# Loading w_down's 64 partitions with six DMAs of 4, 4, 4, 2, 2 and 48 rows in place of eight DMAs of 8 rows

## The chip, the cores and the metric

The kernel runs on one core of a Trainium2 chip. The time is the device time of one execution in microseconds, and the figure to compare is the median of several executions. Before the change it is 2533.44 us (three runs, 2533.29 to 2534.53). A profiled execution also gives a span, from the first to the last instruction, which is a little shorter than the device time.

## The reference

One token is sent through two blocks, and the results are mixed by a gate. Block A is attention over a cache of 65,536 positions with 32 heads of 128; block B is a SwiGLU feed-forward with F = 1792:

```python
q = (x @ wq).reshape(B, Sq, H, Dh).transpose(0, 2, 1, 3)          # 32 heads of 128, one query
p = softmax(einsum("bhqd,bhkd->bhqk", q, k_cache) * Dh ** -0.5)
a = einsum("bhqk,bhkd->bhqd", p, v_cache)  ->  (1, 1, 4096) @ wo   # wo 4096 x 512
b = (silu(x @ w_gate) * (x @ w_up)) @ w_down                       # w_down 1792 x 512
g = sigmoid((x * gate_w).sum(-1, keepdims=True))
out = g * a + (1 - g) * b
```

Everything is bf16. The two caches are 32 x 65536 x 128 values each, 537 MB each, so more than 98% of the bytes that the kernel reads are K and V. w_down is 1.8 MB.

## The kernel before, in words

**Tiles.** A head's 65,536 positions are cut into G = 4 chunks of 16,384, so there are N = 128 chunks. A chunk of K or V is one tile of 128 partitions with 128 positions of 128 values in each: 32 KB per partition, 4 MB in all, loaded by one DMA (`load`, line 108). All large tiles come from one ring of five buffers (`ring`, `SLOTS = 5`), and the same ring holds, at the start, `wq_t`, the two matrices of the feed-forward's input (`gu_t`), and w_down (`wd_t`); at the end it holds the second half of wo.

**The steps.** The loop at line 355 goes through `steps`, one K chunk n and, four or more steps later, one V chunk v. For a K chunk VectorE multiplies K by the query (line 240) and halves the products three times by adding (line 244), until 16 partial sums per position are left; TensorE adds these up with an identity matrix (`scores`, line 254). When a head's four chunks are there, the maximum, the exponentials and the row sum follow (lines 266 to 288). For a V chunk TensorE multiplies the probabilities by V (`values`, line 302).

**The feed-forward.** It is done in the first steps: `feed_forward_in` after step 1 (`gu_ps`, line 176), `feed_forward_mid` in step 2, `feed_forward_out` in step 3. In `feed_forward_mid` TensorE rearranges the hidden vector from 128 partitions of 14 to 64 partitions of 28 (line 202) and then multiplies it by w_down in 28 matmuls (`b_ps`, line 209). w_down stands on 64 partitions for that, each with 28 rows of 512: 28 KB in one run, both in memory and in the tile. These 28 matmuls need all of w_down.

**The order of the DMAs.** All loads but x's are issued by SyncE, in the order of the program, on one hardware queue whose packets are carried by 16 DMA engines. A load of a ring buffer waits until the buffer's last reader is done. Besides, the DMAs take turns on eight completion semaphores, so that each DMA is issued only when the eighth one before it has landed. The order at the start is: wq, K chunk 0 in two halves, K chunk 1, w_gate, w_up, gate_w, two DMAs of w_down (`load_wd(0, 1)`), K chunk 2, six DMAs of w_down (`load_wd(2, ..., 7)`, line 359), K chunk 3, a piece of wo, K chunk 4, V chunk 0, and so on. The buffer of w_down is taken next by K chunk 5.

**w_down's DMAs before.** `load_wd` (line 142) takes rows `lo, lo + 4, ..., lo + 28` for each of eight values of `lo`, so each DMA moves 8 partitions that lie 4 apart, 28 KB each.

Of the kernel before, what the change touches and what calls it, by code (L numbers as in the profile page):

```python
# [25 lines left out]
def kernel(  # L26
# [75 lines left out]
    def load(dst, cache, n, name, cuts=(0, NB)):  # L102
        h, g = divmod(n, G)
        t = big(name)
        view = t.rearrange("p (j d) -> p j d", d=Dh)
        src = cache[0, h, g * NB * P : (g + 1) * NB * P, :].rearrange("(p j) d -> p j d", j=NB)
        for a, b in zip(cuts[:-1], cuts[1:]):
            nc.sync.dma_start(out=view[:, a:b, :], in_=src[:, a:b, :])
        dst[n] = view
# [31 lines left out]

    def load_wd(*which):
        for i in which:
            lo = (0, 1, 2, 3, 32, 33, 34, 35)[i]
            part = slice(lo, lo + 29, 4)
            nc.sync.dma_start(out=wd_sb[part], in_=wd_rows[part])

    with nc.allow_non_contiguous_dma(reason="small"):
# [8 lines left out]
    def load_wo_end(cuts):  # L157
        t = big("wo_t")[:, : (H - WH) * D].rearrange("p (h n) -> p h n", n=D)
        rows = A_wo[WH * P :, :].rearrange("(h p) n -> p h n", p=P)
        for a, b in zip(cuts[:-1], cuts[1:]):  # L160
            nc.sync.dma_start(out=t[:, a:b, :], in_=rows[:, a:b, :])
        wo_end.append(t)

    def load_wo(g):
        wo_tiles[g] = wo_pool.tile([P, WG, D], bf16, name="wo_sb")
        rows = A_wo[g * WG * P : (g + 1) * WG * P, :]
        nc.sync.dma_start(out=wo_tiles[g], in_=rows.rearrange("(h p) n -> p h n", p=P))

    def feed_forward_in():

        gu_ps = psum_m.tile([P, 2 * FT], f32, name="gu_ps", tag="misc")
        for w in range(2):
            cols = wgu_sb[:, w].rearrange("p t (m c) -> p t c m", c=FT)
            for ft in range(FT):
                for t in range(KT):
                    nc.tensor.matmul(
                        gu_ps[:, w * FT + ft : w * FT + ft + 1],
                        lhsT=cols[:, t, ft, :],
                        rhs=xT[:, t : t + 1],
                        start=(t == 0),  # L180
                        stop=(t == KT - 1),
                    )
        gu_sb = consts.tile([P, 2 * FT], f32, name="gu_sb")
        nc.scalar.activation(out=gu_sb, in_=gu_ps, func=ACT.Copy)
        eg = consts.tile([P, FT], f32, name="eg")
        nc.scalar.activation(out=eg, in_=gu_sb[:, :FT], func=ACT.Exp, scale=-1.0)
        return gu_sb, eg

    def feed_forward_mid(gu_sb, eg):
        nc.vector.tensor_scalar_add(eg, eg, 1.0)  # L190
        nc.vector.reciprocal(eg, eg)
        hprod = consts.tile([P, FT], f32, name="hprod")
        nc.vector.tensor_tensor(out=hprod, in0=gu_sb[:, :FT], in1=eg, op=ALU.mult)
        hT = consts.tile([P, FT], bf16, name="hT")
        nc.vector.tensor_tensor(out=hT, in0=hprod, in1=gu_sb[:, FT:], op=ALU.mult)
        xg = consts.tile([P, KT], f32, name="xg")
        nc.vector.tensor_tensor(out=xg, in0=xT, in1=gwT, op=ALU.mult)
        xs = consts.tile([P, 1], f32, name="xs")
        nc.vector.tensor_reduce(out=xs, in_=xg, axis=AXIS.X, op=ALU.add)
        h_ps = psum_m.tile([HP, GT], f32, name="h_ps", tag="misc")  # L200
        for r in range(2):
            nc.tensor.matmul(
                h_ps[:, r * FT : (r + 1) * FT], lhsT=ident_b[:, r::2], rhs=hT, start=True, stop=True
            )
        h2 = consts.tile([HP, GT], bf16, name="h2")
        nc.scalar.activation(out=h2, in_=h_ps, func=ACT.Copy)
        b_ps = psum_m.tile([1, D], f32, name="b_ps", tag="misc")
        for t in range(GT):
            nc.tensor.matmul(  # L209
                b_ps, lhsT=h2[:, t : t + 1], rhs=wd_sb[:, t, :], start=(t == 0), stop=(t == GT - 1)  # L210
            )
        g_ps = psum_m.tile([P, 1], f32, name="g_ps", tag="misc")
        nc.tensor.matmul(g_ps, lhsT=ones_f, rhs=xs, start=True, stop=True)
        eg2 = consts.tile([P, 1], f32, name="eg2")
        nc.scalar.activation(out=eg2, in_=g_ps, func=ACT.Exp, scale=-1.0)
        return b_ps, eg2
# [13 lines left out]
    def products(n, a=0, b=NB):  # L230

        h = n // G
        K = K_tiles[n][:, a:b, :]
        qb = q_bc[:, h * Dh : (h + 1) * Dh]
        q_rep = bass.AP(
            tensor=qb.tensor,
            offset=qb.offset,
            ap=[list(qb.ap[0]), [0, b - a], [1, Dh]],
        )
        yield nc.vector.tensor_tensor(out=K, in0=K, in1=q_rep, op=ALU.mult)  # L240
        half = Dh
        while half > WIDTH:
            half //= 2
            yield nc.vector.tensor_tensor(  # L244
                out=K[:, :, 0:half], in0=K[:, :, 0:half], in1=K[:, :, half : 2 * half],
                op=ALU.add,
            )
# [15 lines left out]
    def row_max(h):  # L263

        m = small.tile([P, 1], f32, name="m")
        nc.vector.tensor_reduce(out=m, in_=S_tiles[h], axis=AXIS.X, op=ALU.max)  # L266
        diag = small.tile([P, P], f32, name="diag")
        nc.scalar.activation(out=diag, in_=ident_f, func=ACT.Copy, scale=m)  # L268
        mT_ps = psum_m.tile([P, P], f32, name="mT_ps", tag="misc")
        nc.tensor.matmul(mT_ps, lhsT=ones_f, rhs=diag, start=True, stop=True)  # L270
        return mT_ps

    def exponentials(h, mT_ps):
        top = small.tile([P, 1], f32, name="top")
        nc.vector.tensor_reduce(out=top, in_=mT_ps, axis=AXIS.X, op=ALU.max)  # L275
        bias = small.tile([P, 1], f32, name="bias")
        nc.scalar.activation(out=bias, in_=top, func=ACT.Copy, scale=-scale)
        P_tiles[h] = ppool.tile([P, NBH], bf16, name="P_sb")
        nc.scalar.activation(  # L279
            out=P_tiles[h], in_=S_tiles[h], func=ACT.Exp, bias=bias, scale=scale,  # L280
            accum_out=rowsum[:, h : h + 1],
        )
        del S_tiles[h]
# [71 lines left out]
    for n, v in steps:  # L355
        if n is not None and n > 1:
            load(K_tiles, A_k_cache, n, "K_t")
        if n == 2:
            load_wd(2, 3, 4, 5, 6, 7)
        if n == 3:  # L360
            load_wo(0)
        if v is not None:
            if v % (WG * G) == 2 * G and v // (WG * G) + 1 < WH // WG:
                load_wo(v // (WG * G) + 1)
            load(V_tiles, A_v_cache, v, "V_t", (0, NB) if v < N - 2 else (0, 64, NB) if v < N - 1 else (0, 32, 64, 96, 112, NB))
            if v == N - 1:
                load_wo_end((0, 4, 8, 12, 14, 16))
        if n == 2:
            ff = feed_forward_mid(*ff)
        halves = (0, NB // 2)  # L370
        vector = iter(()) if n is None else products(n)
        if n == 0:
            vector = (i for a in halves for i in products(n, a, a + NB // 2))
        top_of = None
        if n is None:
            top_of = H - 1 if S_tiles else None
        elif n % G == 0 and n > 0:
            top_of = n // G - 1
            vector = (i for a in halves for i in products(n, a, a + NB // 2))
        if top_of is not None:  # L380
            next(vector, None)
            mT_ps = row_max(top_of)
            next(vector, None)
            exponentials(top_of, mT_ps)
        for _ in vector:
            pass
        if n == 1:
            ff = feed_forward_in()
        if n == 3:
            feed_forward_out(*ff)  # L390
        if tot_ps is not None:
            weight(*tot_ps)
            tot_ps = None
        if done is not None:
            head_column(done, head_copy(done))
        if v is not None:
            values(v)
        if top_of is not None:
            tot_ps = top_of, total(top_of)
        if n is not None:  # L400
            scores(n)
        if done is not None and done < WH:
            project(done)
        done = v // G if v is not None and v % G == G - 1 else None
# [40 lines left out]
```

## Time and profile before

| | |
|---|---|
| median of three runs | 2533.44 us |
| the profiled execution | 2534.51 us, span 2532.6 us |
| VectorE busy | 2175.5 us (86%) |
| TensorE busy | 1742.4 us (69%) |
| read from memory | 1087.64 MB, 429 GB/s over the span |
| V loads of 4096 KB, issue to landing (median) | 29.1 us |
| K loads of 4096 KB, issue to landing (median) | 35.3 us |
| 28 matmuls with w_down | 12.1 us, from 60.35 us on |

In the views of the profile, "L302" is line 302 of the kernel, "DVE" is VectorE, "PE" TensorE, "ACT" ScalarE and "SPq" the queue of SyncE, which issues the DMAs. "V_t<-in_A_v_cache_dram" reads: tile V_t from the input A_v_cache. A DMA's "landing" is the moment at which its last engine has reported completion. Each engine that takes part in a DMA reports it with a small packet of four bytes of its own, and these marks, with their times, are in the trace's records beside the packets of data. In the view by windows, the columns after each engine's busy time give the granted clock of TensorE, the mean busy share of the 16 DMA engines, and GB/s.

### The profile page before, as it was taken

The numbers are of one execution on the slowest core, as the hardware profiler recorded it, in microseconds if no ns is written. First come the engines' busy times: TensorE is split into PE (matmuls) and PEld (weight loads), VectorE is DVE, ScalarE is ACT, GpSimd is POOL, SyncE is SP. The second block draws the span as 40 slices with busy tenths as digits, with TensorE's granted clock in tenths as the row PEclk, the third lists the DMA queues.
The fourth block names the chain that finished last, engine by engine and source line by source line (L and its number), as shares of the span: only waits on it lengthen the run. The fifth ranks groups of instructions, "written<-read, shape, count | busy, mean of one in ns | idle before, by whom it ended". The sixth has DMA issues, their size and how long they took to land.

```text
span 2532.6 us, 15260 instructions
## 1 busy us (share of the span) xinstructions
PE 1742.4 (69%) x6738; PEld 712.1 (28%) x6738; DVE 2175.5 (86%) x784; ACT 75.9 (3%) x207; POOL 0.7 (0%) x6
## 2 busy tenths in 40 slices
PE   4677666776677666676776677667666776677679
PEld 2222222222222222222222223222222232222223
DVE  7998888888888999998888888888888888888860
ACT  1000000000000000000000000000000000000000
POOL 0000000000000000000000000000000000000000
PEclk7677777777777676677777777777777777777779
DMA  9999999999999999999999999999999999999998
GB/s 415 433 433 430 433 433 433 432 430 435 432 432 434 431 433 432 432 433 433 432 434 433 432 434 433 432 432 434 432 431 434 433 430 434 434 431 433 434 432 339
DMA packets 42884, 1088.63 MB, mean 430 GB/s; under 512 B 4737, under 2 KB 8834, under 8 KB 9090
## 3 DMA queue, kind: packets, MB, share of 16 engines
q1 hardware_dynamic: 42674, 1087.66, 99.7%
q8 instruction: 53, 0.87, 0.1%
q14 instruction: 13, 0.11, 0.0%
q10 hardware_dynamic: 144, 0.00, 0.0%
HBM read 1087.64 MB, written 0.00 MB: 429 GB/s over the span
## 4 chain that ended last, share of the span: by engine, by line
DMA 68%; PE 22%; DVE 10%; issue 1%; ACT 0%; DVEq 0%; SPq 0%
DMA V_t<-in_A_v_cache_dram 61%; PE O_ps L302 20%; DMA K_t<-in_A_k_cache_dram 5%; DVE K_t L240 5%; DVE K_t L244 5%; PE S_ps L254 1%; DMA wo_t<-in_A_wo_dram 1%; DMA wq_t<-in_A_wq_dram 0%; PE qg_ps L117 0%; DVE m L266 0%; PE oh_ps L323 0%; PE a_ps L335 0%; PE a_ps L227 0%; ACT P_sb L279 0%; DVE top L275 0%
## 5 line engine op out<-in xcount | busy, mean ns | idle before, releaser
L302 PE MATMUL O_ps<-V_t,P_sb 128*4 128x512 bf16 x4096 | 1157.3, 453 | 496.8 <-DMA V_t<-in_A_v_cache_dram 494.3
L240 DVE TENSOR_TENSOR K_t<-K_t,q_bc 128x16384 bf16<-128x16384 bf16 (+1 forms) x160 | 1117.2, 6983 | 254.4 <-DMA K_t<-in_A_k_cache_dram 232.9
L244 DVE TENSOR_TENSOR K_t<-K_t 128x4096 bf16<-128x4096 bf16 (+3 forms) x480 | 1030.9, 2148 | 14.3
L302 PEld LDWEIGHTS <-P_sb 128*4 128x4 bf16 x4096 | 393.9, 97 | 1241.0 <-issue 897.5
L254 PE MATMUL S_ps<-K_t,ident_b 128*128 128x128 bf16 x2048 | 466.0, 394 | 107.0 <-DVE K_t L244 106.9
L254 PEld LDWEIGHTS <-ident_b 128*128 128x128 bf16 x2048 | 227.6, 115 | 330.0 <-issue 140.2
L323 PE MATMUL oh_ps<-ident_f,O_sb 4*128 4x1 f32 x256 | 57.9, 343 | 74.1 <-ACT O_sb L315 74.1
L323 PEld LDWEIGHTS oh_ps<-ident_f,O_sb 4*128 4x128 f32 x256 | 55.2, 314 | 83.7 <-ACT O_sb L315 78.9
L270 PE MATMUL mT_ps<-diag,ones_f 128*128 128x128 f32 x64 | 23.6, 468 | 79.8 <-ACT diag L268 79.8
L268 ACT ACTIVATE diag<-ident_f,m 128x128 f32<-128x128 f32 x32 | 12.8, 401 | 2099.3 <-DVE m L266 2099.3
L317 DVE COPY O_sb<-O_ps 4x256 f32<-4x256 f32 x1 | 0.4, 414 | 52.1 <-ACT O_sb L315 52.1
L270 PEld LDWEIGHTS mT_ps<-diag,ones_f 128*128 128x128 f32 x64 | 14.7, 285 | 95.6 <-ACT diag L268 95.6
L266 DVE TENSOR_REDUCE m<-S_ps 128x1 f32<-128x512 f32 x32 | 21.9, 683 | 7.4 <-PE S_ps L254 7.4
L315 ACT ACTIVATE O_sb<-O_ps 4x512 f32<-4x512 f32 (+1 forms) x32 | 18.1, 566 | 131.0 <-PE O_ps L302 131.0
L279 ACT ACTIVATE P_sb<-S_ps,bias 128x512 bf16<-128x512 f32 x32 | 22.0, 687 | 1.0
L117 PE MATMUL qg_ps<-wq_t,X_bc 128*128 128x512 bf16 x32 | 8.6, 436 | 13.2 <-DMA wq_t<-in_A_wq_dram 13.2
L293 DVE RECIPROCAL recip<-tot_ps 128x1 f32<-128x1 f32 x32 | 5.1, 160 | 12.2 <-PE tot_ps L288 12.2
L209 PE MATMUL b_ps<-wd_t,h 64*1 64x512 bf16 x28 | 12.1, 629 | 4.3 <-DMA K_t<-in_A_k_cache_dram 4.3
L288 PEld LDWEIGHTS tot_ps<-rowsum,ones_f 128*128 128x128 f32 x64 | 9.5, 188 | 14.0 <-issue 14.0
L288 PE MATMUL tot_ps<-rowsum,ones_f 128*128 128x1 f32 x64 | 12.2, 260 | 0.0
L330 ACT ACTIVATE oT<-oh_ps,rg 128x1 bf16<-128x1 f32 x32 | 8.4, 263 | 76.6 <-PE oh_ps L323 76.6
L227 PE MATMUL a_ps<-b_sb,ones_f 1*1 1x512 f32 x2 | 1.9, 1032 | 12.1 <-ACT b_sb L226 12.1
(42 smaller groups left out, 73.8 us busy)
## 6 DMA issues: line engine op xcount, KB each, us to landing
K_t<-in_A_k_cache_dram SPq DMA_DIRECT2D x127, 4096.0 KB, 35.3
V_t<-in_A_v_cache_dram SPq DMA_DIRECT2D x126, 4096.0 KB, 29.1
wq_t<-in_A_wq_dram SPq DMA_DIRECT2D x1, 4096.0 KB
K_t<-in_A_k_cache_dram SPq DMA_DIRECT2D x2, 2048.0 KB, 16.8
V_t<-in_A_v_cache_dram SPq DMA_DIRECT2D x2, 2048.0 KB
V_t<-in_A_v_cache_dram SPq DMA_DIRECT2D x3, 1024.0 KB, 29.4
wo_sb<-in_A_wo_dram SPq DMA_DIRECT2D x4, 512.0 KB, 17.3
gu_t<-in_B_w_gate_dram SPq DMA_DIRECT2D x1, 1792.0 KB
```

Of the source, the lines that this page charges most:

```text
L209: nc.tensor.matmul(b_ps, lhsT=h2[:, t : t + 1], rhs=wd_sb[:, t, :], start=(t == 0), stop=(t == GT - 1))
L240: yield nc.vector.tensor_tensor(out=K, in0=K, in1=q_rep, op=ALU.mult)
L244: yield nc.vector.tensor_tensor(out=K[:, :, 0:half], in0=K[:, :, 0:half], in1=K[:, :, half : 2 * half], op=ALU.add,)
L254: nc.tensor.matmul(S_tiles[h][:, g * NB : (g + 1) * NB], lhsT=ident_b, rhs=K_tiles[n][:, :, c], start=(c == 0), stop=(c == WIDTH - 1),)
L266: nc.vector.tensor_reduce(out=m, in_=S_tiles[h], axis=AXIS.X, op=ALU.max)
L268: nc.scalar.activation(out=diag, in_=ident_f, func=ACT.Copy, scale=m)
L270: nc.tensor.matmul(mT_ps, lhsT=ones_f, rhs=diag, start=True, stop=True)
L279: nc.scalar.activation(out=P_tiles[h], in_=S_tiles[h], func=ACT.Exp, bias=bias, scale=scale, accum_out=rowsum[:, h : h + 1],)
L288: nc.tensor.matmul(tot_ps, lhsT=ones_f, rhs=rowsum[:, h : h + 1], start=True, stop=True)
L302: nc.tensor.matmul(O_tiles[h], lhsT=P_tiles[h][:, g * NB + j : g * NB + j + 4], rhs=V_tiles[n][:, j : j + 4, :], start=(g == 0 and j == 0) ...
L315: nc.scalar.activation(out=O_sb[:, :cut], in_=O_ps[:, :cut], func=ACT.Copy)
L323: nc.tensor.matmul(oh_ps, lhsT=O_sb[:, c * Dh : (c + 1) * Dh], rhs=ident_f[0:4, c : c + 1], start=(c == 0), stop=(c == 3),)
```

## The change

w_down's 64 rows are cut in another way: rows 48 to 51, 52 to 55 and 56 to 59 by a DMA of four rows each, rows 60 and 61, and 62 and 63, by a DMA of two rows each, and rows 0 to 47 by one DMA of 48. The first two (48 to 51 and 52 to 55) stand where the first two stood, ahead of K chunk 2, and the other four stand behind it. The same bytes go to the same places in the tile, and nothing else in the kernel differs; each of the engines has the same instructions in the same order, apart from SyncE's two issues fewer.

```diff
     def load_wd(*which):
         for i in which:
-            lo = (0, 1, 2, 3, 32, 33, 34, 35)[i]
-            part = slice(lo, lo + 29, 4)
+            part = slice(*((48, 52), (52, 56), (56, 60), (60, 62), (62, 64), (0, 48))[i])
             nc.sync.dma_start(out=wd_sb[part], in_=wd_rows[part])
...
         if n == 2:
-            load_wd(2, 3, 4, 5, 6, 7)
+            load_wd(2, 3, 4, 5)
```

## The prediction

> **What bounds the kernel now.** I read the head of the page, its forty slices and its chain first, then the table of DMA queues and issues, then the stretch from 0 to 100 us in order of time, then the last 30 us in narrow windows, and last the trace's own packet and semaphore records, which the page does not print and whose numbers I give in words.
>
> ```profile
> span 2532.6 us, 15260 instructions
> PE 1742.4 (69%) x6738; PEld 712.1 (28%) x6738; DVE 2175.5 (86%) x784; ACT 75.9 (3%) x207; POOL 0.7 (0%) x6
> DMA  9999999999999999999999999999999999999998
> DMA packets 42884, 1088.63 MB, mean 430 GB/s; under 512 B 4737, under 2 KB 8834, under 8 KB 9090
> q1 hardware_dynamic: 42674, 1087.66, 99.7%
> q8 instruction: 53, 0.87, 0.1%
> DMA 68%; PE 22%; DVE 10%; issue 1%; ACT 0%; DVEq 0%; SPq 0%
> ...
> V_t<-in_A_v_cache_dram SPq DMA_DIRECT2D x126, 4096.0 KB, 29.1
> wd_t<-in_B_w_down_dram SPq DMA_DIRECT2D x8, 224.0 KB
> ```
>
> No compute engine is full (VectorE 86%), while queue q1 fills 99.7% of 16 DMA engines for the whole span: the time is bytes over the rate of the DMA engines, and an average of 430 GB/s hides which engine is last. A 32 KB packet takes 1213 ns in nearly every record, one of w_down's 28 KB packets 1062 ns in all 64: 27.0 GB/s per engine, 16 times 27 = 432. So a row of w_down costs the engine that carries it 1.06 us, and the question is which engine ends last.
>
> How many engines a DMA uses can be counted: q1 has 4465 four-byte packets, the completion marks. 275 loads of 128 rows at 16 each, eight of 8 rows at 8 each and the one-row output make 4400 + 64 + 1 = 4465. So eight rows go to eight engines, one row each. It is the same eight every time: the K load before w_down's two first pieces lands on all sixteen within 0.73 us, the K load issued at 43.20 us lands on eight engines at 60.1 to 60.5 us and on the other eight at 68.4 to 70.0 us. The 8.3 us between are 8 rows x 1.06 = 8.5 us.
>
> That lead stays to the end. The last V piece (issued 2494.42) lands at 2507.0 (2 engines), 2513.8 to 2514.9 (6), 2515.4 to 2515.6 (4), 2516.2, 2519.8, 2522.6 and 2523.7. Followed back, the first eight are those without w_down. The rest of the spread is q8: each of its 53 instruction fetches of 16 KB stretches a 32 KB packet from 1213 to about 1700 ns, and the lengths repeat with a period of eight, so eight engines take them in turn, 6 or 7 each, and lose some 7 us: six of the eight without w_down and two with it, which are the last two. The windows of the tail show that few engines set the end (share times 16 is the number still moving data):
>
> ```profile
> core 0: us, PE busy (x) PEld busy (x) DVE busy (x) ACT busy (x) POOL busy (x), PEclk, DMA share, GB/s
> 2507.00:2513.00 6.00, 6.00 (x30) 2.34 (x29) 0.00 (x0) 0.00 (x0) 0.00 (x0) 1.00 0.90 379
> 2519.00:2522.00 3.00, 3.00 (x15) 1.19 (x14) 0.00 (x0) 0.00 (x0) 0.00 (x0) 1.00 0.23 88
> 2525.70:2527.90 2.20, 2.20 (x15) 1.34 (x14) 0.23 (x1) 0.26 (x1) 0.00 (x0) 1.00 0.16 53
> ```
>
> From 2519 to 2522 us 0.23 x 16, three to four engines, are left; from 2525.7 two; the last mark is at 2529.1, and the output follows.
>
> **The change, part by part.** Times are against the profiled execution, 2534.51 us (span 2532.6 and 1.9 around it); it lies 1.1 us above the median of 2533.44, and I add the difference to the median.
>
> Issue. Two of eight DMA issues on SyncE go, 2 x 0.62 us (the issues from 22.98 to 42.46 us). Cost nothing: SyncE waits there anyway, each of these issues for the DMA eight earlier on its semaphore. The K load behind them goes out at about 42 instead of 43.20 us, while 10 us of the K load before it is still to come.
>
> ```profile
> 21.86 0.34 SPq L108 DMA_DIRECT2D K_t<-in_A_k_cache_dram  x1
> 22.98 20.11 SPq L146 DMA_DIRECT2D wd_t<-in_B_w_down_dram  x6
> 43.20 0.37 SPq L108 DMA_DIRECT2D K_t<-in_A_k_cache_dram  x1
> ...
> 54.01 8.69 DVE L240 TENSOR_TENSOR K_t<-K_t,q_bc 128x16384 bf16<-128x16384 bf16 x1 [0.80 <-DMA K_t<-in_A_k_cache_dram]
> 60.35 12.10 PE L209 MATMUL b_ps<-wd_t,h 64*1 64x512 bf16 x28 [4.28 <-DMA K_t<-in_A_k_cache_dram]
> ```
>
> Rows per engine. By the counts above (128 rows on 16 engines, 8 on 8, 1 on 1) I take 4 rows on four engines, 2 on two, 48 on sixteen with three each. With the first engines always the same: engines 0 and 1 carry 3 + 2 + 3 = 8 rows, as now; 2 and 3 carry 6; 4 to 7 carry 3; 8 to 15 carry 3 instead of none. By rows alone that is 0, -2.1, -5.3 and +3.2 us. [...]
>
> Where the rows land. Now the eight rows of a piece lie four partitions apart (0, 4, ... 28), and in the large loads each engine writes eight rows of its own, so no record shows two engines writing neighbouring rows. After the change four engines write four neighbouring rows (48 to 51) at once, while the K stream goes on. Bound below: they do not disturb each other, 1.06 us per piece. [...] The nearest row for two streams on one path is the fetch beside a 32 KB packet: 1213 becomes 1700, the two add up and do not overlap. As every packet size runs at the same 27 GB/s, I hold that for a path's limit and take turns. For engines 0 and 1 that is 3 x 5.3 + 2 x 3.2 (two engines and a third) + at most 8.5 (eight rows of the 48 go to each low group) = 30.8 us; I take 28.5, since strangers' rows arrive partly while these engines are held elsewhere. With no K rows in the way it is 3 x 4.25 + 2 x 2.1 + 3.2 = 20.2 us. Today it is 8.5. So +20.0 us for engines 0 and 1 (11.7 to 22.3), some 16 to 18 for 2 and 3, 3 to 7 for the others.
>
> [...]
>
> What waits for that. The K load of step 2 lands at 65 to 69 instead of 53.9 us and that of step 3 at about 90 instead of 70, so VectorE, which starts on them at 54.01 and 70.67, stands still for about 19 us; it idles 233 us for K loads in all, and catches up. w_down is whole at about 80 instead of 60.3 us; the 12.1 us of b_ps on TensorE end at about 92, and behind them the scores of step 2 and the K load that takes w_down's buffer (issued at 72.48 now). Cover: engines 0 and 1 then still hold that K load's two predecessors and end them at about 110, so 18 us are to spare; beyond that every microsecond would be one of the end. The engines that are ahead run dry, at no cost: the last one sets the landing.
>
> Sum. An engine with w_down and without fetches is 8.2 us ahead of the last one (2515.5 against 2523.7). If engines 0 and 1 are such, the end moves by 20.0 - 8.2 = +11.8 us (bounds 3.5 and 14.1): 2533.4 + 11.8 = 2545.2 us.
>
> **The rivals.**
> 1. Turns as above, but one of engines 0 and 1 takes the fetches: +20.0, 2553.4 us (bounds 2545.1 and 2555.7). For it: two of eight are so. Against it: the records carry no engine numbers. With the engine at 2519.8 among them it is +16.
> 2. Faster: no turns, and the two last engines are among 4 to 7. They shed five rows: 5.3 us, the end 2528.1. The eight without w_down go from at most 2514.9 to 2518.1, under 2523.7 - 5.3 = 2518.4, so this gain is whole. It decides if a four-row piece takes less than about 1.5 us. For it: engine load is what bounds the kernel. Against it: the sharing row above.
> 3. No change: no turns, and the last engine is 0 or 1, which carries eight rows before and after: 2533.4; among 2 and 3, 2531.3. The change then does what it says, on engines that do not set the end.
> 4. Turns that are worse than equal, holding up other packets too: above 2556.
>
> **How the numbers follow.** Forecast 0.42; rival 1 0.33; rival 2 0.10; rival 3 0.10; rival 4 0.05. The time is that of the forecast, 2545 us. From 2533 (rival 3) to 2556 (end of rival 1) the range leaves out rivals 2 and 4 and a part of 3, under 0.2. The forecast alone: 2537 to 2548. A measurement of this kernel can tell about 0.2%, 5.1 us. Faster 0.10 (rival 2), same 0.12 (rival 3 and the low edge of the forecast), slower 0.78.
>
> **What the profile after would show.** Right: packets of w_down of 3 to 5 us instead of 1062 ns; the marks of the K load of step 3 spread over some 25 us; b_ps starting near 80 us; VectorE idle ahead of the products of steps 2 and 3; at the end only two to four engines moving data for more than 10 us. Wrong: 1062 ns in all 64 packets (turns fall; rivals 2 or 3, told apart by whether the last marks come 5 us sooner); a spread at step 3 that closes later, if the engines held up find slack I don't see.

## The result and the profile after

The changed kernel takes 2547.43 us (median of four runs, 2546.80 to 2548.38) against 2533.36 us before (four runs): a ratio of 1.0050, 95% interval 1.0039 to 1.0062, or 14.1 us more. The forecast was 2545 us, 2533 to 2556.

The head of the page of the changed kernel, and its rate in forty slices of 63.7 us:

```profile
span 2546.6 us, 15257 instructions
PE 1734.5 (68%) x6738; PEld 710.7 (28%) x6738; DVE 2175.8 (85%) x784; ACT 75.9 (3%) x207; POOL 0.7 (0%) x6
...
DMA  9999999999999999999999999999999999999998
GB/s 339 381 434 429 435 431 434 431 434 430 435 431 433 433 431 435 431 434 432 434 433 432 434 430 434 433 432 433 432 434 431 434 432 432 436 430 433 433 433 372
```

The 16 DMA engines are as busy as before, and the loss is all in the first two slices: 339 and 381 GB/s, then 430 and more to the end. (339 and 381 against 432 over 63.7 us each are 13.7 + 7.5 = 21 us; the start of the program costs 2.8 us of it in both kernels.) So an engine that is busy there moves less: its packets take longer.

Narrower windows of that stretch, first the kernel before, then the changed one (the last two columns are the busy share of the DMA engines and GB/s):

```profile
40.00:50.00 10.00, 5.88 (x99) 5.82 (x98) 9.93 (x3) 0.41 (x2) 0.00 (x0) 0.50 1.04 441
50.00:55.00 5.00, 2.77 (x13) 1.60 (x13) 4.03 (x9) 0.00 (x0) 0.00 (x0) 0.50 0.99 427
55.00:75.00 20.00, 15.72 (x47) 5.47 (x46) 19.90 (x5) 0.36 (x2) 0.00 (x0) 0.50 1.02 435
75.00:80.00 5.00, 1.47 (x7) 0.61 (x5) 4.96 (x2) 0.00 (x0) 0.00 (x0) 0.50 0.98 419
```

```profile
40.00:50.00 10.00, 5.74 (x96) 5.68 (x96) 9.93 (x3) 0.41 (x2) 0.00 (x0) 0.50 1.07 153
50.00:55.00 5.00, 2.91 (x14) 1.69 (x14) 2.91 (x8) 0.00 (x0) 0.00 (x0) 0.50 0.99 423
55.00:75.00 20.00, 0.94 (x6) 0.33 (x4) 7.69 (x1) 0.19 (x1) 0.00 (x0) 0.50 1.00 179
75.00:80.00 5.00, 1.02 (x3) 0.36 (x4) 4.97 (x2) 0.00 (x0) 0.00 (x0) 0.50 0.97 396
```

From 40 to 50 us run the first two pieces of four rows, from 50 to 55 only K chunk 2, and from 55 us on the other four pieces, whose last mark comes at 78.8 us. With the pieces the sixteen engines together move 153 and 179 GB/s; between them, 423. I use one figure for this below, the *loss per engine*: from 40 to 84 us, the bytes short of 432 GB/s, divided by 432, with each packet counted by the part of it that lies in that time (the table counts a packet whole in the window where it begins). It is 0.2 us before and 19.1 us after (in this table, (432 - 153) x 10 / 432 = 6.5 and (432 - 179) x 20 / 432 = 11.7).

In order of time, the changed kernel's waits for that:

```profile
42.62 0.35 SPq L108 DMA_DIRECT2D K_t<-in_A_k_cache_dram  x1
67.31 8.69 DVE L239 TENSOR_TENSOR K_t<-K_t,q_bc 128x16384 bf16<-128x16384 bf16 x1 [14.23 <-DMA K_t<-in_A_k_cache_dram]
78.98 12.10 PE L208 MATMUL b_ps<-wd_t,h 64*1 64x512 bf16 x28 [23.04 <-DMA wd_t<-in_B_w_down_dram]
88.60 8.69 DVE L239 TENSOR_TENSOR K_t<-K_t,q_bc 128x16384 bf16<-128x16384 bf16 x1 [4.55 <-DMA K_t<-in_A_k_cache_dram]
91.11 0.33 SPq L108 DMA_DIRECT2D K_t<-in_A_k_cache_dram  x1
```

VectorE stands still for 14.23 + 4.55 = 18.8 us ahead of chunks 2 and 3, b_ps starts at 78.98 instead of 60.35 us, and the load that takes w_down's buffer goes out at 91.11 instead of 72.48 us. From 80 us on the rate is whole again, so that load was not late.

**Who was held.** The packets of w_down take 3.5 us in the median (1.06 to 4.68), against 1.06 before. But the engines that have nothing to do with a piece are held too: beside the first piece's four packets, begun at 40.3 to 40.5 us, stand twelve 32 KB packets begun at 40.3 to 40.7, and these take 3.6 to 4.9 us instead of 1213 ns; the longest K packet of this stretch takes 5.4 us. The marks carry no engine number; which engine is which is read from the rows it carries and from its lag, which can be followed from load to load. K chunk 2, which has only the first two pieces (engines 0 to 3) ahead of it, landed before the change at 50.4 to 50.9 us on the eight engines without w_down; now eleven engines land it between 57.4 and 58.9 us. K chunk 3 lands at 82.0 to 88.5 us; before at 60.1 to 60.5 on eight engines and 68.4 to 70.0 on eight. So every engine lost 14 to 22 us, and the spread between them fell from 9.9 to 6.5 us. Most of the difference is rows. Taking the marks in order (the twelve first as the engines that now have three rows, then two with six, then two with eight), and counting 1.06 us for each row gained or shed, what is left on the mean is 19.0 us for engines 8 to 15, 19.0 for 4 to 7, 19.1 for 2 and 3, and 19.5 for 0 and 1: all sixteen were held alike.

**The end.** The last V piece landed at 2507.0 to 2523.7 us, on the mean of the sixteen engines at 2515.2; it now lands at 2527.5 to 2537.6, 2533.9 on the mean. The mean is 18.7 us later, the last engine only 13.9: it was 8.5 us behind the mean and is 3.7 us behind it now. The change does even out the engines, by 4.8 us, and pays 18.7 us for it. The windows of the tail of the changed kernel show it:

```profile
2533.00:2536.00 3.00, 3.00 (x16) 1.17 (x15) 0.00 (x0) 0.00 (x0) 0.00 (x0) 1.00 0.77 288
2541.00:2542.50 1.50, 1.50 (x8) 0.57 (x8) 0.00 (x0) 0.26 (x1) 0.00 (x0) 1.00 0.40 130
```

Shortly before the last mark (2543.0 us) 0.40 x 16, about six engines, still move data; at that distance from the end one or two did before.

### The profile page after: what moved, and what is told of

Its sections match the earlier page's. It is cut to its first block, busy times and chain, and to the rows that moved or that the text cites. A ratio compares the mean times of both kernels' runs of the same rounds, so it can differ in the third digit from the quotient of the medians.

```text
span 2546.6 us, 15257 instructions
## 1 busy us (share of the span) xinstructions
PE 1734.5 (68%) x6738; PEld 710.7 (28%) x6738; DVE 2175.8 (85%) x784; ACT 75.9 (3%) x207; POOL 0.7 (0%) x6
## 4 chain that ended last, share of the span: by engine, by line
DMA 69%; PE 21%; DVE 9%; issue 1%; ACT 0%; SPq 0%; DVEq 0%
DMA V_t<-in_A_v_cache_dram 61%; PE O_ps L301 20%; DMA K_t<-in_A_k_cache_dram 6%; DVE K_t L239 4%; DVE K_t L243 4%; DMA gwT<-in_gate_w_dram 2%; PE S_ps L253 1%; DMA wo_t<-in_A_wo_dram 1%; DVE m L265 0%; PE oh_ps L322 0%; PE a_ps L334 0%; ACT P_sb L278 0%; PE a_ps L226 0%; SPq L108 0%; DVE top L274 0%
```

## The experiments

Theory 1, formed from the trace after: engines that write neighbouring partitions at the same time crowd there, and the crowd slows all sixteen engines. Its rivals: that few engines per DMA, neighbouring rows in memory, or the 48-row piece alone cost the time, and that only the writers are held, in turns, as the prediction had it. The edits that take out a line with `lo`, and the last one, are against the kernel before, the others against the changed kernel (the one with `pad` in place of `h2` adds to the run ahead of it); where the number of pieces changes, the calls of `load_wd` change with it and are not shown. Where an expectation says to which partitions an engine's K rows go, that is my assumption: the records name neither engines nor rows. Each ratio below is against runs of the kernel before on the same chip (medians 2534.4 to 2534.6 us).

### Small pieces with their rows four apart

```diff
-            part = slice(*((48, 52), (52, 56), (56, 60), (60, 62), (62, 64), (0, 48))[i])
+            part = slice(*((48, 64, 4), (49, 64, 4), (50, 64, 4), (51, 64, 4), (0, 48))[i])
```

> w_down as four 4-row pieces whose rows lie four apart (48, 52, 56, 60 and so on) and the same 48-row piece. In the changed kernel the total rate falls to 131-175 GB/s from 40 to 50 us, while the first two 4-row pieces run (6.7 us lost), and to 118-262 from 55 to 75 us (11.8 us lost). Theory 1, crowding: engines that write neighbouring partitions together slow all sixteen engines. Then 40 to 50 us is back at about 430 GB/s, only the 48-row piece still loses some 5 us, and the time is 2533 to 2539 us. Rival A, few engines: a DMA on four engines is itself the cost, wherever its rows land. Then 40 to 50 us stays under 200 GB/s, four pieces lose 13 us, and the time is 2545 us or more. Rival B, turns as predicted: only the engines that write into a foreign group are held, 7 to 15 us on engines 0 to 3, and the total rate never falls under 300 GB/s: 2533 to 2548 us.

Measured: 2542.2 us, ratio to before 1.0032 (1.0019 to 1.0045), 7.8 us more. Its windows:

```profile
40.00:50.00 10.00, 5.83 (x98) 5.77 (x97) 9.93 (x3) 0.41 (x2) 0.00 (x0) 0.50 1.03 317
50.00:55.00 5.00, 2.82 (x14) 1.60 (x14) 2.99 (x8) 0.00 (x0) 0.00 (x0) 0.50 1.15 306
55.00:75.00 20.00, 3.27 (x12) 1.15 (x11) 12.55 (x2) 0.19 (x1) 0.00 (x0) 0.50 0.98 245
```

No theory had it whole. The same number of engines with the same bytes loses 3.0 us from 40 to 52 us where neighbouring rows lost 7.1 in that time, so few engines are not the whole cause. But 317 is not 430, where theory 1 had no loss. The small number of engines alone doesn't make the 3.0 us: the run of `Which engines end last` below, whose pieces are four rows four apart on four engines as well, but at rows 0 to 15 and 32 to 47 of the tile, loses 0.3 us in all. Nor do rows 48 to 63 alone: the kernel before writes them four apart too, in pieces on eight engines, and loses 0.2 us. It is the two together, and why isn't shown. The loss per engine is 13.4 us.

### Large piece with its rows four apart

```diff
-            part = slice(*((48, 52), (52, 56), (56, 60), (60, 62), (62, 64), (0, 48))[i])
+            part = slice(*((48, 52), (52, 56), (0, 48, 4), (56, 60), (60, 62), (62, 64), (1, 48, 4), (2, 48, 4), (3, 48, 4))[i])
```

> The three 4-row and two 2-row pieces as in the change, rows 0 to 47 in four pieces of 12 rows that lie four apart. Theory 1: the small pieces keep their loss (6.7 us from 40 to 50 us, some 6 more behind K chunk 2), the large ones lose nearly nothing: 2541 to 2546 us. Rival C, the 48-row piece is what costs: the small pieces show no loss and the time is 2533 us or less.

The first of the four large pieces stands ahead of K chunk 2 here.

Measured: 2544.4 us, ratio 1.0042 (1.0027 to 1.0057), 10.0 us more; 151 GB/s from 40 to 50 us, 274 from 55 to 75; loss 14.2 us per engine. The small pieces keep their loss; the 48-row piece is not the only cause. Rows four apart are cheaper here too, since the loss is 4.9 us less than the change's.

### The 48-row piece alone

```diff
-    load_wd(0, 1)
...
-            load_wd(2, 3, 4, 5)
+            load_wd(0)          # part = slice(0, 48)
```

> The 48-row piece of the change alone, behind K chunk 2; rows 48 to 63 aren't loaded and the products use rows 0 to 31. It tells the small pieces' share of the 19.1 us that the changed kernel lost per engine (16 engines, against 432 GB/s) from the large one's. By the difference of the runs so far (13.4 us lost with four spaced small pieces, 3.0 of it from 40 to 52 us for two of them) the 48 rows alone lose about 7 us, the small ones 12. Every engine then spends 3.2 + 7 us, against 8.5 of engines 0 to 7 before: the last ones end 2 us later, 2535 to 2537 us. If the loss is from small pieces that hold up the large one: under 3 us lost, and 2531 us or less.

Measured: 2537.92 us, ratio 1.0013 (1.0004 to 1.0022); the loss is 8.3 us per engine, where 7 was expected, and it begins with the piece (40 to 50 us at 428 GB/s, 50 to 55 at 167). So of the change's 19.1 us the large piece makes some 8 by itself and the five small ones, by difference, some 11, though these carry a quarter of the bytes.

### Neighbouring partitions, rows far apart in memory

```diff
             part = slice(*((48, 52), (52, 56), (56, 60), (60, 62), (62, 64), (0, 48))[i])
+            rows = slice(*((0, 64, 16), (1, 64, 16), (2, 64, 16), (4, 64, 32), (5, 64, 32), (0, 48))[i])
-            nc.sync.dma_start(out=wd_sb[part], in_=wd_rows[part])
+            nc.sync.dma_start(out=wd_sb[part], in_=wd_rows[rows])
```

> The changed kernel, but the five small pieces take rows of w_down that lie far apart in memory (0, 16, 32, 48; 1, 17, 33, 49; 2, 18, 34, 50; 4, 36; 5, 37) and still write the neighbouring partitions 48 to 63; so b is computed with wrong rows. If the crowd is at the partitions written: 108-154 GB/s again from 40 to 48 us and about 14 us over the kernel before. If it is neighbouring rows in memory: 40 to 48 us near 430 GB/s, and 6 to 10 us less than the changed kernel.

Measured: 2548.15 us, ratio 1.0057 (1.0043 to 1.0071), 13.6 us more; 142 GB/s from 40 to 44 us and 104 from 44 to 48; loss 21.8 us. Nothing is won by taking the rows apart in memory: what matters is where they are written. Why the loss is 2.7 us larger than the change's isn't shown.

### Eight engines on neighbouring rows

```diff
-            lo = (0, 1, 2, 3, 32, 33, 34, 35)[i]
-            part = slice(lo, lo + 29, 4)
+            part = slice(8 * i, 8 * i + 8)
```

> Eight DMAs of 8 neighbouring rows (0 to 7, 8 to 15, ...): the same eight engines and the same bytes as before the change, but two groups with four writers each, and the K rows of that group's engine as a fifth. Theory 2, pace of the slowest: while a piece runs, all sixteen engines move at a quarter to a fifth of their rate; 8 x 3.2 to 4.2 us = 25 to 34 us lost by every engine, those without w_down too: 108 GB/s and less in each piece, K chunk 3 lands 25 us later on all, 2559 to 2567 us. Rival B, turns: only engines 0 to 7 lose 25 us, the other eight land K chunk 3 at 60 us as before, and 16 engines together stay above 230 GB/s; the time is the same, about 2559 us, so the records decide.

Measured: 2553.53 us, ratio 1.0075 (1.0061 to 1.0088), 19.0 us more; loss 17.3 us. Its windows:

```profile
40.00:50.00 10.00, 5.85 (x98) 5.79 (x98) 9.93 (x3) 0.41 (x2) 0.00 (x0) 0.50 1.03 209
55.00:75.00 20.00, 1.04 (x6) 0.43 (x4) 11.43 (x2) 0.19 (x1) 0.00 (x0) 0.50 1.04 208
```

The same eight engines carry the same bytes as before the change; only the order of the partitions differs. K chunk 3 lands at 76.5 to 77.4 us on the eight engines that have no row of w_down at all (before: 60.1 to 60.5), and at 85.7 to 87.5 on the others (68.4 to 70.0). On the mean that is 16.5 us for those that write nothing there and 17.8 for those that do. They did not want for work: K chunk 3 was issued at 49.27 us, before K chunk 2 landed on them (55.7 us and later), and the busy share stays at 1.03 and 1.04 in the windows above. Turns among the writers alone fall: in that theory the first eight land at 60 us. The size of theory 2, in which all engines go at the pace of the slowest, 25 to 34 us, falls as well; it was 2.2 us per piece, not 3.2 to 4.2.

### Sixteen rows per piece, four apart

```diff
-            part = slice(*((48, 52), (52, 56), (56, 60), (60, 62), (62, 64), (0, 48))[i])
+            part = slice(*((0, 64, 4), (1, 64, 4), (2, 64, 4), (3, 64, 4))[i])
```

> All 64 rows in four pieces of 16 rows that lie four apart: each group of four partitions has two engines writing to it in a piece (one of them the engine whose K rows go there), each engine carries 4 rows. Theory 1, if two writers per group don't crowd: no loss of rate, engines with w_down before shed 4.2 us, the others gain 4.2: 2529 us. Theory 1, if two are already a crowd: under 300 GB/s around the pieces and 2535 to 2545 us. Rival B (turns): the second writer is held 8.5 us, the first as before: 2533 us.

Measured: 2536.04 us, ratio 1.0007 (0.9997 to 1.0016): no change that can be told. The loss is 5.3 us, with 342 GB/s from 40 to 50 us and 368 from 55 to 75. The last engine gains from carrying four rows instead of eight, and the loss takes it back. Turns between two engines, each row taking twice its 1.06 us in each of the four pieces, would be 4 x 1.06 = 4.2 us more, as an estimate; the loss is little above that, but that two engines met there isn't shown.

```diff
-            part = slice(*((48, 52), (52, 56), (56, 60), (60, 62), (62, 64), (0, 48))[i])
+            part = slice(0, 64)
```

> w_down as one DMA of 64 rows, four per engine. If an engine takes four neighbouring rows, each group of four partitions has two writers, as with sixteen rows four apart, and the time is that of that run. If an engine takes every sixteenth row, four engines write each of four groups at once: by theory 1 the rate falls under 200 GB/s for some 10 us and the time is 2540 us or more; by rival B engines of the low groups are held 12 us: 2537 to 2545 us.

Measured: 2536.74 us, ratio 1.0010 (1.0001 to 1.0020), loss 5.6 us: nearly that of the run before, and not the 2540 us or more expected if an engine takes every sixteenth row. So I take it that an engine has four neighbouring rows of the 64 here; the records don't name the rows.

### Which engines end last

```diff
-            part = slice(lo, lo + 29, 4)
+            part = slice(lo, lo + 13, 4)
```

> As before the change, but each piece holds only its first four rows, so engines 0 to 3 carry 8 rows each into partitions of their own and engines 4 to 7 none; the products use rows 0 to 15 alone, half of w_down isn't loaded. Which engines end last: in the changed kernel's marks the two engines with 8 rows keep a constant 6.1 and 6.9 us to the first one, while eight others climb from 0-2 to 8.4 us, and one with 6 rows from 3.9 to 10.1 us. If so, engines 4 to 7 hold the two last ones of the kernel before, they shed 8.5 us, and the end is set by that engine of 2 and 3, 3.9 us sooner than before: 2529.5 to 2530.5 us. If the last ones are among 0 to 3: no change.

Measured: 2530.59 us, ratio 0.9985 (0.9976 to 0.9994), 3.9 us less, and a loss of 0.3 us. The last V piece lands at 2520.1 us on the last engine and at 2515.5 or sooner on the fifteen others. Engines 4 to 7 did hold the two late ones. The pieces go to four engines here, as the first two of the change do, but with their rows four apart at rows 0 to 15 and 32 to 47: four engines per DMA alone cost nothing that can be seen.

### w_down on 128 partitions

One DMA of 128 rows of 14 KB, as many rows as a K load has:

```diff
-    HP = P // 2
+    HP = P
...
-            part = slice(*((48, 52), (52, 56), (56, 60), (60, 62), (62, 64), (0, 48))[i])
+            part = slice(0, P)
...
-        for r in range(2):
-            nc.tensor.matmul(
-                h_ps[:, r * FT : (r + 1) * FT], lhsT=ident_b[:, r::2], rhs=hT, start=True, stop=True
-            )
-        h2 = consts.tile([HP, GT], bf16, name="h2")
-        nc.scalar.activation(out=h2, in_=h_ps, func=ACT.Copy)
+        h2 = hT
```

> w_down on 128 partitions with 14 rows of 512 each in one DMA: every engine writes 8 x 14 KB into partitions that its K rows go to as well. 28 matmuls become 14, and the rearranging of the hidden vector goes. No crowd: the rate stays near 430 GB/s. The engines that had w_down shed half of 8.5 us, the others gain as much: the two last engines end 4.2 us sooner, the latest of the others 4.2 us later, 2519.1 to 2519.4 in place of 2523.7 at the last V piece: 4.2 us less than before, about 2530 us. If the hold is not a matter of partitions but of any load at this place: no gain.

Measured: 2540.85 us, ratio 1.0025 (1.0015 to 1.0035), slower by 6.3 us, against the forecast of 4.2 us less. The rate around w_down was whole (loss 0.5 us), so no crowd. But the whole run was slower by a little, as windows far from w_down show, here of the kernel before and then of this one:

```profile
400.00:800.00 400.00, 278.13 (x1054) 112.81 (x1055) 349.49 (x126) 12.29 (x35) 0.00 (x0) 0.75 1.00 433
```

```profile
400.00:800.00 400.00, 283.42 (x1057) 113.42 (x1058) 347.46 (x124) 10.84 (x31) 0.00 (x0) 0.74 1.00 431
```

433 and 431 GB/s: the 32 KB packets took 1213 ns before, and 1215 (half of them) to 1222 here. Dropping the 56-byte tile `h2` had moved the large buffers by 64 bytes. Two runs to test that:

```diff
+        pad = consts.tile([P, 2 * FT], bf16, name="pad")   # in place of h2
+        nc.vector.memset(pad, 0.0)
```

> w_down on 128 partitions in one DMA as in the run before, with an unused tile of 56 bytes per partition in place of the tile that the run had dropped. The run without it lost nothing around w_down (423 GB/s and more from 40 to 84 us but for one slice), yet each 32 KB packet took 1215 to 1222 ns instead of 1213 through the whole run, 0.4 us per 100 us and 9.4 us in all. Dropping the tile had moved all large buffers from byte 30976 (121 x 256) of a partition to 30912, 64 bytes beside a multiple of 256. If that is the cause: packets of 1213 ns again, and 4.2 us less than before the change, 2529 to 2530.5 us. If the width is the cause (all engines in step): 1215 to 1222 ns again and some 2541 us.

Measured: 2530.65 us, ratio 0.9985 (0.9976 to 0.9994), 3.9 us less than before the change: faster than both kernels. The packets are at 1213 ns again, the loss around w_down is 0.2 us, and the last V piece lands at 2520.0 us on the last engine. Its windows around w_down:

```profile
40.00:50.00 10.00, 5.86 (x98) 5.80 (x98) 9.93 (x3) 0.41 (x2) 0.00 (x0) 0.50 1.01 429
55.00:75.00 20.00, 9.42 (x36) 3.78 (x34) 19.90 (x5) 0.17 (x1) 0.00 (x0) 0.67 1.01 432
```

```diff
+    pad = consts.tile([P, 32], bf16, name="pad")           # ahead of rowsum, in the kernel before
+    nc.vector.memset(pad, 0.0)
```

> The kernel before, with 64 bytes per partition more ahead of the large buffers, so that these begin at byte 31040, 64 beside a multiple of 256. If the place of the buffers is what lengthened the packets: 1215 to 1222 ns, and about 9 us more, 2542 to 2544 us. If not: no change.

Measured: 2544.9 us, ratio 1.0039 (1.0023 to 1.0054), 10.3 us more for 64 bytes, with half of the packets at 1215 ns and a fifth at 1222.

## Why the prediction was right, and where it was not

**Issue.** Right: K chunk 3 is issued at 42.62 us (some 42 expected), and nothing waits for it.

**Rows per engine.** Right. The marks count so: queue q1 has 4433 of them now, 4400 of the 128-row loads, 1 of the output, and 4 + 4 + 4 + 2 + 2 + 16 = 32 of w_down (64 before). In the changed kernel two engines land K chunk 3 some 6.0 and 6.5 us behind the first, two more 3.5 and 3.9 us: five and three rows of 1.06 us more than the engines with three. It stays so: the two with eight rows are 6.1 and 6.9 us behind the first at the last V piece as well.

**Turns.** Nearly right in size for the engines that they were worked out for: packets of 3 to 5 us were expected and 3.5 us is the median; K chunk 3 was expected on engines 0 and 1 at about 90 us, and lands at 88.1 and 88.5, 19 us later than before, where the sum had 20. The 5.3 us per piece in that sum, five times the 1.06 us of a row, and its 3.2 and 4.25, three and four times, stand for engines that take turns, one row after another; no run shows such turns. (Packets of 28 and 32 KB move at 27.0 GB/s by their medians in the kernel before, those of 16 KB at 26.8, of 4 KB at 25.8 and of 1 KB at 22.) What the runs showed in their place: the first two pieces' packets took mostly 3.3 to 4.7 us, but engines that wait for no turn were held as long, and with eight neighbouring rows per piece, so again four engines on each four rows, the packets of w_down took 2.8 us in the median.

**Whom the turns hold.** This is the step that failed: "some 16 to 18 for 2 and 3, 3 to 7 for the others". The others lost 14 us (engines 4 to 7) to 22 us (those without w_down before), as much as the writers, and but for the rows all sixteen lost 19.0 to 19.5 us. Turns among the writers don't say so, and what holds the others isn't shown.

**Which engine ends last.** The forecast took engines 0 and 1 to be without the instruction fetches, and they are: their lag to the first engine is constant, while eight others fall back from 0 to 2 us behind it to 8.4 to 9.8. It also put them last, and they are not. At the last V piece they should have stood at 2515.5 + 20.0 = 2535.5 us and stood at 2533.6 and 2534.4. Last, between 2536.0 and 2537.6, come the eight engines that take TensorE's instruction fetches and one of engines 2 and 3. Rival 1 falls with that; and what happened is the mechanism of rival 4, other packets held up too, to which the prediction gave 0.05, at a lower price than the 2556 us given to it.

**The sum.** 11.8 us were forecast, 14.1 measured. That it came out so near is luck, since the engines that it was worked out for are not those that set the end. It did because the holding of engines 0 and 1 that set the forecast, 20 us less the 8.2 us they were ahead, is close to what all sixteen lost, 18.7 us, less the 4.8 us that the even rows gave back. The even rows are rival 2's gain (5.3 us expected): it was there, and `first_four_only` and `wide_128_pad` show it without the crowd (3.9 us less in each, with losses of 0.3 and 0.2 us).

**What waits.** Right: VectorE idle 18.8 us (about 19), b_ps at 78.98 us (80), the load into w_down's buffer at 91.11 us (92) and not late. Wrong were two signs, both of few engines held far behind the others: the marks of K chunk 3 were to spread over some 25 us and spread over 6.5, and two to four engines were to be left alone for 10 us at the end, where the nine last ones land the last V piece within 1.6 us.

## What to carry to other kernels

In this kernel queue q1 fills 99.7% of the DMA engines' time, and the engine that ends last sets the time: before the change it landed the last V piece at 2523.7 us, the mean of the sixteen at 2515.2. In a kernel like it, count the bytes of each engine, and take instruction fetches into the count. In these runs evening the engines out paid only where the rate around w_down stayed whole: 3.9 us less on 128 partitions with the loss at 0.2 us (`wide_128_pad`). A quarter of a 1.8 MB load, written by two or four engines at a time to neighbouring partitions, cost all sixteen some 11 us. And a small tile added or dropped can move the large buffers, which cost 10.3 us for 64 bytes here: look at the length of a large packet whenever a change far from the loads makes them all slower.

## What was not expected of the hardware

Engines that carry no row of w_down are held nearly as long as those that do (16.5 and 17.8 us with eight neighbouring rows per piece). What they share isn't shown. The loss per piece was 3.5 us with four neighbouring rows (7.1 us for the change's first two pieces), 2.2 with eight neighbouring rows (17.3 for eight pieces), 1.5 with four rows four apart among rows 48 to 63 (3.0 for two), and 1.3 with sixteen rows four apart (5.3 for four); no rule for these sizes came out of the runs, and pace of the slowest is not it.

Large buffers that begin at byte 30912 or 31040 of their partition instead of 30976 take 1217.9 to 1218.0 ns per 32 KB packet on the mean (from 200 us on) instead of 1214.0, 0.3%; in the kernel before that cost 10.3 us. No other places were run, and why the two cost time isn't shown; it is the written side of the loads that moved.

The fetches of TensorE's instructions (queue q8: 53 of 16 KB, one for about 254 of its 13,476 instructions; between two fetches it begins 147 to 292) go to eight of the sixteen DMA engines in turn: a fetch stretches a 32 KB packet from 1213 to some 1674 to 1764 ns, and these lengths repeat with a period of eight. Two of the eight are among engines 4 to 7, as `first_four_only` shows (3.9 us less), and the eight fall some 7 us behind over the run (in the changed kernel from 0 to 2 us behind the first engine to 8.4 to 9.8).
